# Products without a reader in the opening of a Fourier-mixing and SoLU kernel, with exponents, table zeros and a mean row moved

## The chip, the cores and the metric

The kernel runs on one core of one Trainium2 chip. The metric is the device time of one execution in microseconds (us). A profile is one execution recorded instruction by instruction; its times count from the start of its span. The engines are TensorE (PE, with its weight loads listed apart as PEld), VectorE (DVE), ScalarE (ACT), GpSimd (POOL) and SyncE (SP, whose queue issues most DMAs).

## The reference

For x of shape 8 x 3136 x 256, each batch is Fourier transformed over the sequence and over the features, and the real part is kept. Each of the 25,088 rows then passes a small network:

```
X = fft(fft(x, axis=1), axis=2).real          # rows of 256
h = X @ w_in                                   # 256 x 1024
e = exp(h - max(h));  solu = h * e / sum(e)
ln = (solu - mean) / sqrt(var + 1e-6) * g_ln   # mean and var over the 1024
out = ln @ w_out                               # 1024 x 256
```

w_in, w_out and g_ln are random. Here w_in and w_out arrive as 64-bit floats, and the kernel converts them to 32 bits itself, in the opening.

## The kernel before

**The work.** The batches are taken in four pairs. For each pair the sequence transform of length 3136 = 49 x 64 is split in two: a first transform over 49 (`transform1`), and a second over 64 (`transform2`). The features' transform is folded into the weights: the kernel computes `Wi`, the product of the Fourier table Q and w_in, once, in the opening. After that it works through 100 units of 128 rows (25 per pair). For each unit PE computes the second transform (L245), ACT copies its result to q (L251), PE multiplies q by `Wi` in an even and an odd half (`up`, L281), DVE joins the halves (L294, L302), ACT takes exponents and squares, DVE the products (L317), and the result is turned and multiplied by `Wo`. The even half needs `w_mid`, a further row of weights.

**The opening.** The first pair is loaded in eight pieces (c = 0 to 7). A piece needs a direct load (xa, or `room` for pieces 2 to 5, issued by SP) and an indexed load of its mirror image (xb, issued by POOL). DVE adds the two (`add_mirror`, L145 and L147), folds the features (`fold`, L152, L153, L165) into a buffer y, of which there are two, so that the fold of piece c + 2 waits until PE has read piece c. `transform1` (L217) multiplies y by the table F in two steps of four calls; each call appears in the profile as two records. ACT copies each step's result (L220), SP stores it to a scratch tensor zd, and when all eight pieces are there, `turn` reads it back as g, which `transform2` needs.

**The weights in the opening.** w_in comes in four pieces of 512 columns (raw_in). `exponent_in(i)` takes a piece's exponents on DVE (L586) and confines them in three steps on ACT (L610, L612, L614, in `confine`); `narrow_in(i)` builds the 32-bit numbers on DVE in four instructions (L586, L627, L630, L636), of which L630 needs the confined exponents. `product_in(h)` (L690) makes the two halves of `Wi` and the middle row on PE, in PSUM tiles of tags h0 and h1; `keep_in` copies them out (L694). w_out is converted in the same way (`exponent_out`, `narrow_out`). `mean_out(0)` (L737) multiplies a matrix of ones by the first half of `Wo`, four calls of 256 columns, and `mean_out(1)` adds the second half later; `keep_mean` copies the sum out as the mean row. `T`, the table of the second transform, is zeroed at L820 before its two blocks are loaded (L675).

**What sets the order.** The schedule is manual: each engine takes its instructions in the order in which the program lists them, and semaphores order them between engines. The loop over c in the main body gives, for each piece: conversion of a piece of w_in (c = 0: pieces 0 and 1, c = 1: piece 2), `add_mirror`, in c = 0 and c = 2 the exponents of w_in's pieces 2 and 3, `fold`, in c = 2 the conversion of piece 3, the load of piece c + 6, in c = 3 the issue of w_out's load and of the first table, then `transform1`, and from c = 3 on parts of `product_in`. After the loop come the rest of `product_in`, the last exponents, `mean_out(0)`, and for units 0 and 1 `transform2`, `take2` (L251) and `spread`. `begin(i)` issues for a unit both calls of `up` with `even` (L294) between them, and `second_transform(i + 2)`. The loop over units calls `begin(1)` after the exponentials of unit 0 and before its product.

Of the kernel before, what the change touches and what calls it, by code (L numbers as in the profile page):

```python
# [9 lines left out]
FP32 = mybir.dt.float32  # L10
# [7 lines left out]
P = 128  # L18
# [26 lines left out]
def kernel(  # L45
# [19 lines left out]
    nc = tc.nc  # L65
    B, S, D = x.shape
    FF = moe_w_in.shape[1]
# [16 lines left out]
    ps_h = ctx.enter_context(tc.tile_pool(name="ps_h", bufs=1, space=PSUM))  # L84
# [11 lines left out]
    ident = const.tile([P, P], FP32, name="ident")  # L96
# [21 lines left out]
    def load(pr, c, room=None):  # L118

        r = slice(pr.p * PR, (pr.p + 1) * PR)  # L120
        rows = PR if pr.p else P
        if room is None:
            xa = xpool.tile([P, CH, D], FP32, tag="xa", name="xa")
            xb = xpool.tile([P, CH, D], FP32, tag="xb", name="xb")
        else:
            xa, xb = (t.rearrange("p (l d) -> p l d", d=D) for t in room)
        nc.sync.dma_start(out=xa[0:rows], in_=x_pn[r.start : r.start + rows, c * CH + 1 : (c + 1) * CH + 1, :])
        i = pr.p * NC + c
        nc.gpsimd.indirect_dma_start(
            out=xb[0:rows].rearrange("p l d -> p (l d)"), out_offset=None, in_=x_g,  # L130
            in_offset=bass.IndirectOffsetOnAxis(ap=idx[0:rows, i : i + 1], axis=0))
        xa, xb = xa[0:PR], xb[0:PR]
        x0 = None
        if c == NC - 1:
            x0 = xpool.tile([PR, 1, D], FP32, tag="x0", name="x0", bufs=1)
            nc.sync.dma_start(out=x0, in_=x_pn[r, 0:1, :])
        pr.raw[c] = (xa, xb, x0)

    def add_mirror(pr, c, engine, part=None):

        xa, xb, _ = pr.raw[c]
        rows = (0, CH) if part is None else (part * CH // 2, (part + 1) * CH // 2)
        r = slice(rows[0], min(rows[1], CH - 1 if c == NC - 1 else CH))
        a, rb = xa[:, r, :], xb[:, ::-1, :][:, r, :]
        i = engine.tensor_tensor(out=a[:, :, 1:D], in0=a[:, :, 1:D], in1=rb[:, :, D - 1 : 0 : -1], op=ALU.add)  # L145
        if part is None:
            engine.tensor_tensor(out=a[:, :, 0:1], in0=a[:, :, 0:1], in1=rb[:, :, 0:1], op=ALU.add)  # L147
        return i
# [6 lines left out]
    def fold(pr, c):  # L155

        xa, _, x0 = pr.raw.pop(c)
        pr.y[c] = xpool.tile([PR, CH, D], FP32, tag="y", name="y")
        sides = [(pr.y[c], xa)]
        if c == NC - 1:  # L160
            pr.y0 = xpool.tile([PR, 1, D], FP32, tag="y0", name="y0", bufs=1)
            sides.append((pr.y0, x0))
        for o, i in sides:
            fold_features(o, i)
            nc.vector.tensor_copy(out=o[:, :, 0:129:128], in_=i[:, :, 0:129:128])  # L165
# [406 lines left out]
    NW = 512  # L572
# [25 lines left out]
    def confine(unit, here=False, parts=(0, 1, 2)):  # L598

        if unit is None:  # L600
            return
        if here:
            bits(unit, unit, -896.0, ALU.add, 0.0, ALU.max)
            bits(unit, unit, 255.0, ALU.min, 2.0 ** 23, ALU.mult)
            return

        u = unit.bitcast(FP32)
        for i in parts:
            if i == 0:
                nc.scalar.activation(out=u, in_=unit, func=ACT.Relu, bias=limits[:, 0:1])  # L610
            elif i == 1:
                nc.scalar.activation(out=u, in_=u, func=ACT.Relu, bias=limits[:, 1:2], scale=-1.0)  # L612
            else:
                nc.scalar.activation(out=unit, in_=u, func=ACT.Identity, bias=limits[:, 2:3], scale=-(2.0 ** 23))  # L614
# [24 lines left out]
    class Weights:  # L639
# [43 lines left out]
        def product_in(self, h, parts=range(4), ps=None):  # L683
# [6 lines left out]
                nc.tensor.matmul(ps[:, fs], lhsT, self.w_in[c][:, fs], start=(c == 0), stop=(c == KD - 1))  # L690
            return ps

        def keep_in(self, h, ps):
            nc.scalar.copy(w_mid if h == KD else Wi[:, h, :], ps)  # L694

# [95 lines left out]
    with tc.manual_schedule():  # L791
        pairs = [Pair(p) for p in range(NP)]
        first, weights = pairs[0], Weights()
# [23 lines left out]
        for i, limit in enumerate((-896.0, 255.0, 255.0 * 2.0 ** 23, 1e-12)):  # L817
            nc.vector.memset(limits[:, i : i + 1], limit)
        for t in T:
            nc.vector.memset(t, 0.0)  # L820
        weights.exponent_in(0)
        weights.exponent_in(1)
        for c in range(NC):

            if c == 0:
                weights.narrow_in(0)
                weights.narrow_in(1)
            elif c == 1:
                weights.narrow_in(2)
            add_mirror(first, c, nc.vector)  # L830
            if c in (0, 2):
                weights.exponent_in(2 + c // 2)
            fold(first, c)
            if c == 2:
                weights.narrow_in(3)
            if c == NC - 1:
                for i in range(2):
                    weights.exponent_out(i)
                confine(weights.units[0], True)
                weights.narrow_out(0)  # L840
            if c + 6 < NC:
                load(first, c + 6)
            if c == 3:
                weights.place_out()
                for i in range(2):
                    weights.load_out(i)
                weights.load_table(0)
                weights.scale_out()
            for s in range(CH // 2):
                if c == NC - 1:  # L850
                    confine(weights.units[0], parts=(s,))
                transform1(first, c * CH // 2 + s)
            if c == 3:
                weights.mid()
                weights.keep_in(0, weights.product_in(0))
            elif c == 4:
                odd = weights.product_in(1, (0,))
            elif c == 5:
                weights.product_in(1, (1,), odd)
# [13 lines left out]
        units = [Unit(p, k1) for p in range(NP) for k1 in range(NK)]  # L873
        for i in (1, 2):
            weights.narrow_out(i)
        weights.mean_out(0)
        pairs_q = [(t, transform2(pairs[0], t.k1, t.k1)) for t in units[:2]]
        confine(weights.units[0], parts=(0, 1))
        for (t, ps), part in zip(pairs_q, ((2,), ())):
# [29 lines left out]
        def begin(i):  # L909

            cur = units[i]
            enter(i)
            ps = up(cur, 0)
            if i in (2, 3):
                column(cur)
            even(cur, ps)
            cur.odd = up(cur, 1)
            second_transform(i + 2)

        def other_pairs(i, do, *a):  # L920
            cur = units[i]
            if cur.p + 1 < NP:
                do(pairs[cur.p + 1], i, *a)

        batches = []
        begin(0)
        for i in range(whole + 1):
            cur = units[i]
            prv = units[i - 1] if i else None
            if prv:  # L930
                turn_whole(prv, i == 1)
            if i == 1:
                weights.mean_out(1)
            for s in cur.signs:
                join(cur, s)
            if i == 0:
                weights.narrow_out(3, (2,))
                weights.fold_out()
            if 1 < i < whole:
                for o, ps in prv.wait:  # L940
                    nc.vector.tensor_copy(out=o, in_=ps)
            for s in cur.signs:
                expo(cur, s)
            if i == 1:
                weights.keep_mean()
            if i in (1, whole):
                for o, ps in prv.wait:
                    nc.scalar.copy(o, ps)
            if i == 0:
                begin(1)  # L950
            done = units[0 if i == 2 else i - 1 : i] if i > 1 else []
            for t in done:
                stats(t)
            if i == whole:
                nxt = units[i + 1]
                enter(i + 1)
                even(nxt, up(nxt, 0))
            if i == whole:
                other_pairs(i, ahead, "fold")
            for s in cur.signs:  # L960
                product(cur, s)
                if i < whole and s == 0:
                    square(cur, s)
            if i == 1:
                weights.centre(cur)
            if i == 2:
                weight_sums(cur)
            if i < whole:

                if i:  # L970
                    begin(i + 1)
                if 1 in cur.signs:
                    square(cur, 1)
            else:
                for s in cur.signs:
                    square(cur, s)
                other_pairs(i, ahead, "mirror", cur)
                sums(units[1], None, part=slice(2, 4))
                turn_both(cur)
                stats(cur)  # L980
            for work in ("mirror", "fold", "load") if i < whole else ("load",):
                other_pairs(i, ahead, work, cur)
            if i == whole - 1:
                sums(units[1], None, part=slice(0, 2))
            for t in done:
                power(t)
# [185 lines left out]
```

## Time and profile before

| what | value |
|---|---|
| median of three executions | 1125.55 us (1125.4 to 1126.89) |
| the profiled execution | 1126.52 us |
| its span, first to last instruction | 1124.6 us |
| mean granted clock of TensorE | 0.995 of full |
| PE busy | 1093.9 us (97%) |
| DVE busy | 980.1 us (87%) |
| ACT busy | 798.3 us (71%) |
| POOL busy | 802.6 us (71%) |
| first product on PE | 16.44 us |
| first product of `up` | 57.88 us |

In the order of time, a line gives start and length in us, engine, line of the program, operation, output<-input by the program's names, size and number of records, and in brackets the idle time of the engine before it and what ended it. A line with several records is merged: its length reaches from the start of the first to the end of the last. PE's records overlap, so the distance of two starts says more than a length. In a table of stretches, a line gives the stretch, its length, the busy us (and records) of PE, PEld, DVE, ACT and POOL, the clock that TensorE was granted (1.00 is full), the mean busy share of the DMA engines and what they moved in GB/s.

### The profile page before, as it was taken

What the parts mean: (1) busy time and instruction counts of PE and PEld (TensorE: products, weight loads), DVE (VectorE), ACT (ScalarE), POOL (GpSimd) and SP (SyncE); (2) the same over time, 40 slices, a digit from 0 to 9 for tenths busy, and PEclk for the clock granted to TensorE, in tenths of its full rate; (3) what the DMA queues carried; (4) which work ended last, traced back from release to release, by engine and by line L of the source; (5) the groups of instructions that cost most, each with busy time, mean ns of one, the idle gap of its engine ahead of it and who ended that gap; (6) DMA issues with size and microseconds to landing.
All of it is one profiled execution on the core that took longest, in us unless ns stands there. A gap on an engine that the chain in (4) does not pass through costs nothing. (4 is left out here: it accounts for less than half of the span.)

```text
span 1124.6 us, 22003 instructions
## 1 busy us (share of the span) xinstructions
PE 1093.9 (97%) x7031; PEld 874.4 (78%) x7031; DVE 980.1 (87%) x1440; ACT 798.3 (71%) x1946; POOL 802.6 (71%) x707
## 2 busy tenths in 40 slices
PE   3899999999999999999999999999999999999998
PEld 2556878787787787878877787878877788778888
DVE  7899889889889888898888988898988899888984
ACT  4478777777766777777767777777776777777771
POOL 3058888776777888865877788876776676766665
PEclk9899999999999999999999999999999999999999
DMA  9473798766978889766988797776786785865665
GB/s 350 170 202 85 175 188 199 179 145 151 172 174 164 203 178 190 193 146 141 163 171 178 173 194 186 192 178 143 153 154 145 139 163 124 157 145 112 141 136 125
DMA packets 457929, 187.74 MB, mean 167 GB/s; under 512 B 424646, under 2 KB 439254, under 8 KB 457816
## 3 DMA queue, kind: packets, MB, share of 16 engines
q1 hardware_dynamic: 443800, 146.94, 61.7%
q0 software_dynamic: 14016, 39.40, 13.0%
q8 instruction: 57, 0.93, 0.4%
q14 instruction: 56, 0.46, 0.1%
HBM read 46.75 MB, written 38.80 MB: 76 GB/s over the span
## 5 line engine op out<-in xcount | busy, mean ns | idle before, releaser
L281 PE MATMUL ps_h<-Wi,q 128*128 128x512 f32 x800 | 361.6, 593 | 0.5 <-DVE nmax L302 0.2
L457 POOL TENSOR_TENSOR S<-uT 128x512 f32<-128x512 f32 x186 | 237.6, 1278 | 111.0 <-DVE u L317 30.7
L464 PE MATMUL ps_m<-Ws,S 128*128 128x128 f32 x2304 | 296.1, 275 | 0.0
L464 PEld LDWEIGHTS ps_m<-Ws,S 128*128 128x128 f32 x2304 | 279.5, 192 | 3.4 <-DVE S L457 0.2
L324 ACT ACTIVATE h<-u,usum 128x1024 f32<-128x1024 f32 x196 | 224.9, 1148 | 71.5 <-DVE u L317 71.3
L281 PEld LDWEIGHTS ps_h<-Wi,q 128*128 128x128 f32 x800 | 144.2, 190 | 145.0 <-issue 141.9
L317 DVE SCALAR_TENSOR_TENSOR u<-h,u 128x1024 f32<-128x1024 f32 x196 | 232.9, 1224 | 10.7 <-ACT u L310 10.6
L310 ACT ACTIVATE u<-h,nmax 128x1024 f32<-128x1024 f32 x196 | 223.2, 1141 | 2.3 <-DVE nmax L302 1.1
L388 DVE STREAM_TRANSPOSE v<-u 128x2048 f32<-128x2048 f32 x88 | 203.4, 2311 | 3.0
L464 PE MATMUL ps_m<-Wo,uT 128*128 128x128 f32 x1536 | 203.7, 276 | 0.0
L464 PEld LDWEIGHTS ps_m<-Wo,uT 128*128 128x128 f32 x1536 | 187.9, 192 | 1.0 <-issue 1.0
L302 DVE CUSTOM_DVE_ANT_0 h<-ev,ps_h 128x1024 f32<-128x1024 f32 x100 | 122.1, 1221 | 17.1 <-DVE ev L294 9.3
L302 DVE CUSTOM_DVE_ANT_0 h<-h,ps_h 128x1024 f32<-128x1024 f32 x96 | 117.2, 1221 | 14.6 <-DVE nmax L302 0.5
L551 POOL DMA_INDIRECT out_dram<-ot,idx x96 | 107.5, 1120 | 27.6 <-issue 10.2
L457 POOL TENSOR_TENSOR S<-uT,S 128x512 f32<-128x512 f32 x93 | 118.9, 1279 | 7.2
L457 POOL TENSOR_TENSOR S<-S,uT 128x512 f32<-128x512 f32 x93 | 118.7, 1277 | 7.3
L294 DVE SCALAR_TENSOR_TENSOR ev<-w_mid,r,ps_h 128x1024 f32<-128x1024 f32 x99 | 122.8, 1240 | 0.9 <-PE ps_h L281 0.7
L464 PE MATMUL ps_m<-Ws,uT 128*128 128x128 f32 x768 | 101.8, 276 | 0.0
L464 PE MATMUL ps_m<-Wo,S 128*128 128x128 f32 x768 | 101.4, 275 | 0.0
L245 PEld LDWEIGHTS ps_m<-T,g 128*128 128x128 f32 x400 | 60.1, 191 | 47.3 <-issue 45.9
L217 PE MATMUL ps_m<-y,F 98*100 98x258 f32 (+3 forms) x288 | 71.8, 384 | 24.5 <-DVE y L165 22.8
L499 ACT ACTIVATE ot<-ps_m,rs 128x256 f32<-128x256 f32 x96 | 45.5, 474 | 70.6 <-PE ps_m L464 50.6
(111 smaller groups left out, 1232.9 us busy)
## 6 DMA issues: line engine op xcount, KB each, us to landing
uT<-v SPq DMA_DIRECT2D x752, 128.0 KB
g<-zd POOLq DMA_DIRECT2D x72, 160.0 KB, 5.3
out_dram<-ot SPq DMA_DIRECT2D x176, 64.0 KB
zd<-z SPq DMA_DIRECT2D x24, 400.0 KB
xa<-in_x_dram SPq DMA_DIRECT2D x24, 392.0 KB
raw_in<-in_moe_w_in_dram SPq DMA_DIRECT2D x4, 512.0 KB
xa<-in_x_dram SPq DMA_DIRECT2D x4, 512.0 KB
room<-in_x_dram SPq DMA_DIRECT2D x4, 512.0 KB
```

The source lines that it names most:

```text
L217: nc.tensor.matmul(o[..., cs], F[:, 2 * t + h, :], i[..., cs], start=first, stop=True, skip_group_check=True)
L245: nc.tensor.matmul(o, g[:, k, h * P : (h + 1) * P], table, start=(h == 0), stop=True, skip_group_check=True)
L281: nc.tensor.matmul(ps[:, fs], t.q[:, c * P : (c + 1) * P], Wi[:, c, fs], start=True, stop=not whole_even)
L294: nc.vector.scalar_tensor_tensor(out=t.ev, in0=w_mid, scalar=t.r, in1=ps, op0=ALU.mult, op1=ALU.add)
L302: nc.vector.tensor_tensor_reduce(out=t.h[s], in0=t.h[0] if s else t.ev, in1=t.odd, scale=1.0 if s else -0.5, scalar=3.0e38, op0=ALU.add, o ...
L310: nc.scalar.activation(out=t.u[s], in_=t.h[s], func=ACT.Exp, bias=t.nmax[:, s : s + 1], scale=-1.0, accum_out=t.esum[:, s : s + 1])
L317: t.last = nc.vector.scalar_tensor_tensor(out=t.u[s], in0=t.h[s], scalar=-1.0, in1=t.u[s], op0=ALU.mult, op1=ALU.mult, accum_out=t.usum[:, ...
L324: nc.scalar.activation(out=t.h[s], in_=t.u[s], func=ACT.Square, bias=t.usum[:, s : s + 1], scale=-float(FF), accum_out=t.ssq[:, s : s + 1])
L388: nc.vector.transpose(out=t.batch.v[:, :, t.w], in_=t.both.rearrange("p s (g n) -> p (s g) n", n=32))
L457: i = engine.tensor_tensor(out=S[j], in0=a, in1=b, op=op)
L464: nc.tensor.matmul(o, a[:, c], b[:, c], start=start and c == 0, stop=c == n - 1, skip_group_check=True)
L551: dma = nc.gpsimd.indirect_dma_start(out=out, out_offset=bass.IndirectOffsetOnAxis(ap=idx[:, i : i + 1], axis=0), in_=t.ot[s], in_offset=None)
```

## The change

Four edits, all of them in the opening:

- A new function `busy(n)` multiplies `ident` by the first 512 columns of w_in, n times, into a PSUM tile of tag h0. Nobody reads the result. It is called before `transform1` of pieces 0 to 3, with n = 12, 2, 1 and 4.
- `exponent_in(3)` moves from piece 2, between `add_mirror` and `fold`, to piece 1, after `fold`.
- The two zero fills of T move from DVE to GpSimd, at the same place in the program.
- `mean_out(0)` moves from ahead of the first `transform2` to behind `begin(0)`.

```diff
+        def busy(self, n):
+            ps = ps_h.tile([P, FF], FP32, tag="h0", name="busy")
+            for _ in range(n):
+                nc.tensor.matmul(ps[:, 0:NW], ident, self.w_in[0][:, 0:NW], start=True, stop=True)
+
...
         for t in T:
-            nc.vector.memset(t, 0.0)
+            nc.gpsimd.memset(t, 0.0)
...
             add_mirror(first, c, nc.vector)
-            if c in (0, 2):
-                weights.exponent_in(2 + c // 2)
+            if c == 0:
+                weights.exponent_in(2)
             fold(first, c)
-            if c == 2:
+            if c == 1:
+                weights.exponent_in(3)
+            elif c == 2:
                 weights.narrow_in(3)
...
                 weights.scale_out()
+            if c < 4:
+                weights.busy((12, 2, 1, 4)[c])
             for s in range(CH // 2):
...
         for i in (1, 2):
             weights.narrow_out(i)
-        weights.mean_out(0)
         pairs_q = [(t, transform2(pairs[0], t.k1, t.k1)) for t in units[:2]]
...
         begin(0)
+        weights.mean_out(0)
         for i in range(whole + 1):
```

## Prediction

> **What bounds the kernel now.** I read the busy totals first, then the opening alone.
>
> ```profile
> PE 1093.9 (97%) x7031; PEld 874.4 (78%) x7031; DVE 980.1 (87%) x1440; ACT 798.3 (71%) x1946; POOL 802.6 (71%) x707
> ```
>
> TensorE (PE) is busy 1093.9 of 1124.6 us; 22.8 us of its 30.7 idle us are three waits before 32.24 us (16.44, 1.31 and 5.06). So from the end of the opening on, PE has hardly a gap: what the opening loses or wins should reach the end nearly whole. PE in order of time:
>
> ```profile
> 16.44 3.73 PE L217 MATMUL ps_m<-y,F 98*100 98x258 f32 x8 [16.44 <-DVE y L165]
> 21.49 5.54 PE L217 MATMUL ps_m<-y,F 98*100 98x258 f32 x16 [1.31 <-DVE y L165]
> ...
> 32.24 3.71 PE L217 MATMUL ps_m<-y,F 98*100 98x258 f32 x8 [5.06 <-DVE y L165]
> 35.74 5.17 PE L690 MATMUL wps<-w_in,Q 128*128 128x512 f32 x8
> 40.75 1.89 PE L217 MATMUL ps_m<-y,F 98*100 98x258 f32 x8
> ```
>
> The eight records of one piece (L217) take 3.7 us early and 1.89 at 40.75. The clock explains it; here are the busy times and the granted clock in stretches of 3.41 us:
>
> ```profile
> 25.25:28.66 3.41, 1.93 (x9) 1.18 (x8) 0.65 (x1) 3.33 (x6) 0.00 (x0) 1.00 1.03 397
> 28.66:32.07 3.41, 0.00 (x0) 0.00 (x0) 3.35 (x8) 0.35 (x2) 0.00 (x0) 0.50 0.94 366
> 32.07:35.48 3.41, 3.24 (x8) 2.31 (x9) 3.38 (x7) 0.59 (x1) 0.00 (x0) 0.50 0.61 221
> 35.48:38.90 3.42, 3.42 (x6) 1.52 (x5) 2.97 (x7) 1.18 (x3) 0.00 (x0) 0.50 0.97 352
> 38.90:42.31 3.41, 3.41 (x13) 1.94 (x12) 0.00 (x0) 1.36 (x2) 0.00 (x0) 1.00 0.39 141
> 1117.51:1120.93 3.42, 2.49 (x22) 2.29 (x21) 0.83 (x2) 0.53 (x2) 0.96 (x1) 1.00 0.00 0
> ```
>
> A stretch with PE busy 1.93 of 3.41 us was followed by half clock; one with 3.24 at half clock did not bring it back, one with 3.42 did. Near the end 2.49 busy of 3.42 did not lose it. Before 25.25 the column has no record; the 3.73 us of the first piece say half clock. The 5.06 us gap comes from VectorE:
>
> ```profile
> 28.01 0.75 DVE L630 SCALAR_TENSOR_TENSOR S<-raw_in,top_bit,S 128x512 int32<-128x512 int32 x1 [2.84 <-ACT S L614]
> ...
> 42.68 0.69 DVE L152 TENSOR_TENSOR y<-xa 98x508 f32<-98x508 f32 x1 [4.13 <-PE ps_m L217]
> ```
>
> At 28.01 it had waited 2.84 us for the exponents of w_in's last piece, at 42.68 it waits 4.13 us for a y buffer, that is for PE. From 32.24 to 57.8 PE sets the pace. How that stretch ends (PE, then ACT, then DVE):
>
> ```profile
> 51.55 3.60 PE L690 MATMUL wps<-w_in,w_mid 128*128 128x512 f32 x8
> 54.98 1.89 PE L737 MATMUL ps_m<-Wo,ones 128*128 128x256 f32 x8
> 56.71 1.05 PE L245 MATMUL ps_m<-T,g 128*128 128x128 f32 x8
> 57.88 3.70 PE L281 MATMUL ps_h<-Wi,q 128*128 128x512 f32 x8
> ...
> 61.87 3.60 PE L281 MATMUL ps_h<-Wi,q 128*128 128x512 f32 x8
> ```
>
> ```profile
> 55.19 1.01 ACT L694 COPY w_mid<-wps 128x1024 f32<-128x1024 f32 x1 [0.29 <-PE wps L690]
> 56.09 0.72 ACT L610 ACTIVATE S<-S,limits 128x512 f32<-128x512 int32 x1
> 56.85 0.72 ACT L612 ACTIVATE S<-S,limits 128x512 f32<-128x512 f32 x1
> 57.48 0.35 ACT L251 COPY q<-ps_m 128x256 f32<-128x256 f32 x1
> ```
>
> ```profile
> 63.79 1.28 DVE L294 SCALAR_TENSOR_TENSOR ev<-w_mid,r,ps_h 128x1024 f32<-128x1024 f32 x1
> ```
>
> The mean row (L737) fills PE while ScalarE (ACT), without a break after its wait at 55.19, keeps w_mid, does two steps of exponents and then copies q, which `up` (57.88) needs. Without L737, q would still not come before 57.48.
>
> **The skill.** "TensorE: Matmul & The Clock Gate", Part 1, says that the clock is halved until a busy window of about 3.4 us has passed, and that these windows run free of the kernel's start. The trace agrees (0.215 against 0.43 us a record; changes at 25.25, 28.66 and 38.90). Its summary "Why this matters for your kernels" allows PE gaps of up to about 3 us; here 1.5 us idle within one stretch (27.2 to 28.66) was enough, and the measurement decides. The same page (Part 1, engine queue depths) calls ACT and DVE strictly first in, first out: the q copy, queued behind the exponents, agrees. For the memsets, "GPSIMD Engine Reference", 3.1, gives 1.03 cycles an element for one-input bodies (quoted at 1.2 GHz); only a 128x128 memset, 0.21 us, is in the trace.
>
> **The added products.** One call of 512 columns is two records of 0.43 us (0.857), twice that at half clock. The first needs `ident` (1.3 us) and w_in's first 512 columns, written by the L636 step that ends at 9.32; PE starts at 9.37. The counts 12, 2, 1 and 4 are 10.28, 1.71, 0.86 and 3.43 us at full clock: 16.28. With four pieces of `transform1` (4 x 1.72 = 6.88), the gain transpose (0.15) and `product_in(0)` (3.43), PE has 26.74 us of work ahead of piece 4's transform, plus C/2, where C is the time at half clock: from 3.4 (a window begins at 9.37) to 6.8 us, middle 5.1. So piece 4 starts at 9.37 + 26.74 + C/2 = 36.11 + C/2 = 37.8 to 39.5, middle **38.7**, against 40.75: **a gain of 2.05 us** (2.9 to 1.2). This holds if data never come later than PE. The first y is there at 16.44, but the twelve products end at 19.65 + C/2 = 22.2: PE is late, not DVE. Piece 2's fold waits for piece 0's y buffer (two buffers), to 22.2 + 1.9 = 24.1 instead of 22.75. Piece 3's y is there at about 31.0 (next part); PE reaches it at 33.5. So 2.5 us of the added products are pure delay, and they hide every smaller change on DVE.
>
> **Exponents sooner.** The step is one DVE instruction (0.34 us of its row) and three ACT ones (2.25). They move ahead of piece 1's two copies on ACT: these wait until 26.8, but PE finishes piece 1 only at 27.4, so nobody waits for the DMA behind them either. ACT gets to the exponents after piece 0's copies (24.6), is done at 26.8, and DVE's L630, due at 26.55, starts at 26.9; piece 3's y, 4.08 us later as in the trace, comes at 31.0 instead of 32.1. With this edit alone undone, the exponents would follow piece 1's copies (28.1) to 30.3, y would come at 34.4 and cost 0.9 us; as it is, the edit is worth nothing beyond the sum above. On SP's queue, piece 0's store to zd goes from 20.8 to 24.7, and piece 7's load behind it from 21.46 to 25; it landed at 32.8, so some 36.4, and is used after 41.
>
> **Table zeros.** DVE's two memsets (0.59 + 2.19) were followed by a 0.41 us wait for raw_in: nothing gained. On GpSimd they stand behind the index loads (10.65): 3,200 elements are about 2.7 us by the skill's price (an estimate), 8 by the 128x512 additions' 1278 ns. They end between 13.4 and 18.7, so piece 6's indexed load (14.91) slips by 0 to 3.8 us. It lands at 28, is used at 37: worth 0. I take 2.7.
>
> **The mean row later.** Eight records of 0.215, 1.72 us, leave PE ahead of `transform2`; by the ACT rows above this gains 0, since q waits for ACT. Put after `begin(0)`, they lie between the third `transform2` and `up` of unit 1 (61.87). Its first half ends at 63.7, which is when L294 starts (63.79); DVE was free at 63.65. So L294 waits: behind it on DVE are the product of unit 0 and all that follows, and PE's transposes wait for that product. DVE has hardly a gap up to 98 us to make it good. **Cost 1.66 us** (0 if it is made good later).
>
> **Sum.** 1126.52 (profiled run; span 1124.6 and 1.9 around it) - 2.05 + 1.66 = **1126.1**; with C from 3.4 to 6.8, 1125.3 to 1127.0. The profiled run lies 0.97 above the median 1125.55 of three (1125.4 to 1126.89). It got its clock back 6.7 us after 32.24, near the latest phase, and each us there costs 0.5; at another phase the kernel before is up to 1.6 us shorter. Against the median my sum is 0.5 us slower, under the 0.2% (2.25 us) that a measurement can tell from no change.
>
> **Rivals.** *The clock is lost again* (ends slower). With the mean row gone, PE idles from 55.1 until g lands (about 56.2, by the DMA events), and from the end of the two `transform2` (57.3) to 57.88: some 1.7 us of 2.8, all shifted alike. The clock was lost with 1.48 idle us in a stretch and kept with 0.93. Where a window covers most of the gap, half clock follows for one or two windows: 1.7 to 3.2 us, middle 2.4, on `up`, which is on the path. Time 1128.5. It decides if more than about 1.2 idle us in a window is enough, and then for some phases, perhaps half. *The mean row's cost is made good*: PE has about 1.5 idle us between 60 and 100 (38.49 busy of 40 in stretches of ten); then 1126.1 - 1.66 = 1124.4. Against it: DVE's rows follow each other. *The products start later*, after the second half's conversion (11.8) if the wait covers the whole w_in tile: +2.45, 1128.6. Against it: the mean row at 54.98 read Wo while L636 still wrote other columns of it at 56.4.
>
> **How the numbers follow.** Sum as above 0.56; clock lost 0.25; made good 0.12; later start 0.07. Faster by over 0.2% (below 1123.3) needs the made-good case at its luckiest: 0.03. Slower (above 1127.8): 0.25 and 0.05 of the last. The range, 1124.4 to 1128.9, takes in half of the made-good case and most of the slow ones.
>
> **What would show it.** Right: PE busy without a gap from 9.4 to about 53, full clock from 13 to 16 us on, piece 4's L217 at 37.8 to 39.5, L610 to `up` as now, L737 ahead of unit 1's `up`, and L294 of unit 1 waiting some 1.6 us for PE. Wrong: a wait for y in that stretch, q sooner after w_mid than 2.3 us, or unit 1's L294 not waiting.

## The result, and the profile after

The changed kernel takes 1126.88 us (median of 22 executions, 1126.07 to 1130.56), the kernel before 1125.32 (22 executions, 1123.71 to 1126.89). The ratio is 1.0015, 95% interval 1.0009 to 1.0021: 0.15% slower, or 1.56 us. The forecast was 1126.1 (1124.4 to 1128.9), within 0.2% of before; the measured time is 0.8 us above it. The profiled execution of the changed kernel took 1126.33 us (span 1124.6), 0.55 under its median; that of before had taken 1126.52, 1.2 above its own.

PE of the changed kernel in order of time; these lines answer to the L217, L690, L737 and L281 lines of before (L737 is now L742, L694 is L699, and L696 is `busy`):

```profile
9.55 12.75 PE L696 MATMUL busy<-w_in,ident 128*128 128x512 f32 x24 [9.55 <-DVE w_in L636]
22.14 1.89 PE L217 MATMUL ps_m<-y,F 98*100 98x258 f32 x8
...
33.69 1.89 PE L217 MATMUL ps_m<-y,F 98*100 98x258 f32 x8
35.42 3.60 PE L690 MATMUL wps<-w_in,Q 128*128 128x512 f32 x8
38.85 1.89 PE L217 MATMUL ps_m<-y,F 98*100 98x258 f32 x8
...
49.66 3.60 PE L690 MATMUL wps<-w_in,w_mid 128*128 128x512 f32 x8
54.52 1.13 PE L245 MATMUL ps_m<-T,g 128*128 128x128 f32 x8 [1.27 <-DMA g<-zd]
55.99 3.70 PE L281 MATMUL ps_h<-Wi,q 128*128 128x512 f32 x8 [0.34 <-ACT q L251]
59.53 0.61 PE L245 MATMUL ps_m<-T,g 128*128 128x128 f32 x4
59.98 1.89 PE L742 MATMUL ps_m<-Wo,ones 128*128 128x256 f32 x8
61.70 3.60 PE L281 MATMUL ps_h<-Wi,q 128*128 128x512 f32 x8
```

No idle time is listed between 9.55 and the end of L690: PE works without a gap, and every piece takes 1.89 us, the length at full clock. Piece 4 (third L217 line) starts at 38.85 instead of 40.75, and `up` of unit 0 at 55.99 instead of 57.88: 1.9 us sooner. But `up` of unit 1, behind L742, starts at 61.70 instead of 61.87. DVE shows the two ends of this, a wait for a y buffer early and for unit 1's `up` late, with the exponents between them:

```profile
24.07 0.69 DVE L152 TENSOR_TENSOR y<-room 98x508 f32<-98x508 f32 x1 [2.11 <-PE ps_m L217]
...
26.82 0.75 DVE L630 SCALAR_TENSOR_TENSOR S<-raw_in,top_bit,S 128x512 int32<-128x512 int32 x1 [0.33 <-ACT S L614]
```

```profile
60.88 0.88 DVE L636 SCALAR_TENSOR_TENSOR Wo<-raw_out,g_ln,S 128x256 f32<-128x256 f32 x2
63.62 1.28 DVE L294 SCALAR_TENSOR_TENSOR ev<-w_mid,r,ps_h 128x1024 f32<-128x1024 f32 x1 [1.87 <-PE ps_h L281]
```

The 2.84 us wait for the exponents has shrunk to 0.33, yet 2.11 us of waiting for PE stand ahead of it: VectorE did not get ahead; it now waits for TensorE instead of ScalarE. And where L294 of unit 1 followed L636 at once, it now waits 1.87 us. ACT between w_mid and q is as before, only 1.9 us sooner:

```profile
53.29 1.01 ACT L699 COPY w_mid<-wps 128x1024 f32<-128x1024 f32 x1 [0.29 <-PE wps L690]
54.20 0.72 ACT L610 ACTIVATE S<-S,limits 128x512 f32<-128x512 int32 x1
54.96 0.72 ACT L612 ACTIVATE S<-S,limits 128x512 f32<-128x512 f32 x1
55.59 0.35 ACT L251 COPY q<-ps_m 128x256 f32<-128x256 f32 x1
```

From w_mid to q it is 2.30 us, against 2.29 before. Taking the mean row away from PE there has moved nothing.

How much of a shift in the opening reaches the end? For each record of `up` (800 in either kernel) I subtracted its start before from its start in the profile named; the last column is the difference of the two profiled executions' times:

```
us against before   record 1   record 9   record 401   record 800   whole time
changed kernel        -1.89      -0.16       -0.13        -0.13        -0.19
e1, row back          -0.73      -0.73       -0.72        -0.72        -0.77
e2, row late alone    -2.13      +1.30       +1.32        +1.32        +1.25
e3, exponents alone   -3.44      -3.44       -3.42        -3.43        -3.41
e7, fewer, row late   -5.71      -3.99       -3.99        -3.99        -3.46
e9, seven             -6.18      -6.18       -6.17        -6.10        -5.15
```

Record 9 is the first of unit 1. From there on a shift stays to within 0.1 us over a thousand us in these six; only behind the last `up` do two of them give back 0.5 and 1.0. In the profiles of e4 and e6 it moved by 0.1 on the way, in that of e10 by 0.35. So the start of unit 1's `up` tells what a profiled execution is worth, to about 1 us.

### The profile page after: what moved, and what is told of

The parts are those of the page before. It is cut to its first block, busy times and chain, and to the rows that moved or that the text cites. A ratio compares the mean times of both kernels' runs of the same rounds, so it can differ in the third digit from the quotient of the medians.

```text
span 1124.6 us, 22083 instructions
## 1 busy us (share of the span) xinstructions
PE 1105.5 (98%) x7069; PEld 878.8 (78%) x7069; DVE 977.8 (87%) x1438; ACT 798.4 (71%) x1946; POOL 809.2 (72%) x709
## 5 line engine op out<-in xcount | busy, mean ns | idle before, releaser
L281 PE MATMUL ps_h<-Wi,q 128*128 128x512 f32 x800 | 361.6, 593 | 0.7 <-ACT q L251 0.3
L281 PEld LDWEIGHTS ps_h<-Wi,q 128*128 128x128 f32 x800 | 144.3, 190 | 145.3 <-issue 142.2
L294 DVE SCALAR_TENSOR_TENSOR ev<-w_mid,r,ps_h 128x1024 f32<-128x1024 f32 x99 | 122.9, 1241 | 2.7 <-PE ps_h L281 2.6
L464 PEld LDWEIGHTS ps_m<-Ws,uT 128*128 128x128 f32 x768 | 93.8, 192 | 0.0
```

Of the source, the lines that this page charges most:

```text
L281: nc.tensor.matmul(ps[:, fs], t.q[:, c * P : (c + 1) * P], Wi[:, c, fs], start=True, stop=not whole_even)
L294: nc.vector.scalar_tensor_tensor(out=t.ev, in0=w_mid, scalar=t.r, in1=ps, op0=ALU.mult, op1=ALU.add)
L464: nc.tensor.matmul(o, a[:, c], b[:, c], start=start and c == 0, stop=c == n - 1, skip_group_check=True)
```

## The experiments

All ratios are to executions of the kernel before run beside them. The theory is the prediction's sum; the rivals are named in each expectation. e1 to e4, e5 to e8 and e9 to e11 ran on three chips, where the kernel before took 1125.12, 1125.37 and 1125.43 us, so a difference across these groups is rougher than one within.

**e1: the changed kernel with the mean row back in its old place.**

```diff
+        weights.mean_out(0)
         pairs_q = [(t, transform2(pairs[0], t.k1, t.k1)) for t in units[:2]]
...
         begin(0)
-        weights.mean_out(0)
```

> The changed kernel with the mean row back ahead of the first second transform. Theory of the sum (the row was free in the gap that PE has there while ACT copies q, and costs 1.7 us where it stands now, because unit 1's even half on DVE waits for it): 1.75 us less than the changed kernel, about 1125.1, within 0.3 us of the kernel before; up of unit 1 starts 1.7 us sooner after up of unit 0 than in the changed kernel. Rival (the row's cost is made good later; the loss comes from the added products): the time of the changed kernel, about 1126.9.

Measured: 1125.23 us, ratio 0.9999 (0.9990 to 1.0007). It is 1.65 us under the changed kernel's 1126.88 (1.8 by the ratios), and the rest of the change, together, is worth nothing that can be measured. In its profile `up` of unit 1 follows that of unit 0 after 3.98 us (57.16 and 61.14), against 5.71 in the changed kernel. So the sum holds for the row, and the rival, that its cost is made good later, falls.

**e2: the mean row moved, nothing else.**

```diff
-        weights.mean_out(0)
         pairs_q = [(t, transform2(pairs[0], t.k1, t.k1)) for t in units[:2]]
...
         begin(0)
+        weights.mean_out(0)
```

> The kernel before with only the mean row moved behind begin(0). Theory of the sum: 1.7 us slower than before, about 1127.0, with DVE's even half of unit 1 waiting 1.7 to 1.9 us for PE. Rival (made good later): as before, 1125.3. Rival (the clock is lost in the gap before up): 1128 to 1130, with half clock in the records after 57 us.

Measured: 1127.32 us, ratio 1.0023 (1.0016 to 1.0029), 2.2 us above before (1125.12). The move alone costs what was expected and somewhat more. Its profile shows where more can come from; here are PE's last lines of the opening, and three stretches of it (columns as before, the granted clock third from the end):

```profile
49.42 3.60 PE L690 MATMUL wps<-w_in,w_mid 128*128 128x512 f32 x8
54.02 1.13 PE L245 MATMUL ps_m<-T,g 128*128 128x128 f32 x8 [1.00 <-DMA g<-zd]
55.76 5.40 PE L281 MATMUL ps_h<-Wi,q 128*128 128x512 f32 x8 [0.61 <-ACT q L251]
```

```profile
52.77:56.19 3.42, 1.81 (x10) 1.26 (x10) 3.32 (x7) 3.10 (x5) 0.71 (x2) 1.00 0.39 125
56.19:59.60 3.41, 3.41 (x5) 1.35 (x4) 1.18 (x3) 0.40 (x2) 0.00 (x0) 0.50 0.32 60
59.60:63.01 3.41, 3.41 (x16) 2.41 (x15) 2.69 (x5) 0.93 (x2) 0.00 (x0) 1.00 0.64 127
```

A stretch with 1.61 idle us is followed by one at half clock, and `up` of unit 0 takes 5.40 instead of 3.70 us. The prediction's rival of a lost clock is real in this kernel, in this execution. The mean granted clock was recorded for every execution; a stretch of 3.41 us at half clock lowers it by 0.0015 (half of 3.41 in 1125). Nine of the 21 executions have 0.997 and a median of 1126.83, 1.7 us above before; the other twelve have 0.995 or 0.996 and 1127.85. That fits the lost clock, but the gap before piece 3 costs the clock in this kernel too (before itself has 0.995 to 0.997), so the figures don't separate the two losses.

**e3: the exponents of w_in's last piece moved, nothing else.**

```diff
-            if c in (0, 2):
-                weights.exponent_in(2 + c // 2)
+            if c == 0:
+                weights.exponent_in(2)
             fold(first, c)
-            if c == 2:
+            if c == 1:
+                weights.exponent_in(3)
+            elif c == 2:
                 weights.narrow_in(3)
```

> The kernel before with only the exponents of w_in's last piece moved. Theory of the sum (without the added products VectorE sets the pace until piece 3, so the 2.84 us wait at L630 is on the path): the wait is gone, piece 3 reaches PE near 29.3 instead of 32.2, and the time falls by 2.5 to 3.3 us, to about 1122.5. Rival (PE or the loads take the place of that wait, as they do in the changed kernel): within 0.5 us of before.

Measured: 1122.61 us, ratio 0.9977 (0.9969 to 0.9984): 2.5 us faster. The edit that was forecast at nothing beyond the sum in the company of the others is the best of them alone. PE and one line of DVE of its profile:

```profile
28.85 3.71 PE L217 MATMUL ps_m<-y,F 98*100 98x258 f32 x8 [2.23 <-DVE y L165]
32.35 5.12 PE L690 MATMUL wps<-w_in,Q 128*128 128x512 f32 x8
37.30 1.89 PE L217 MATMUL ps_m<-y,F 98*100 98x258 f32 x8
```

```profile
24.63 0.75 DVE L630 SCALAR_TENSOR_TENSOR S<-raw_in,top_bit,S 128x512 int32<-128x512 int32 x1
```

L630 no longer waits. Piece 3 comes 3.4 us sooner than before (28.85 against 32.24), still at half clock (3.71), and that is the shift that stays to the end. Not all of it is due to the exponents: piece 0 came 1.1 us sooner in this execution (15.35 against 16.44), as it did in e2 (15.37), which lacks this edit and reaches piece 3 at 31.16. The 2.3 us between 31.16 and 28.85 agree with the 2.5 of the medians.

**e4: the added products, nothing else.**

```diff
+            if c < 4:
+                weights.busy((12, 2, 1, 4)[c])
             for s in range(CH // 2):
```

> The kernel before with only the added products (12, 2, 1, 4). Theory of the sum: full clock from 13 to 16 us on, but piece 0 reaches PE only at about 22, and the exponents of the last piece come behind piece 1's copies, at 30.3, so that PE waits about 0.9 us for piece 3; the clock won and the time spent nearly cancel: 0.5 us slower than the median of before, about 1125.8 (1125.0 to 1126.5). Rival (the clock alone is worth 1.5 to 2 us of the opening): about 1123.5.

Measured: 1126.56 us, ratio 1.0011 (1.0004 to 1.0018), 1.4 us above before (1125.12) where 0.5 was expected (1125.0 to 1126.5 us). The rival (the clock alone gains) falls. PE and DVE of the profile, whose execution took 1127.52, 1.0 above the median:

```profile
10.93 13.39 PE L696 MATMUL busy<-w_in,ident 128*128 128x512 f32 x24 [10.93 <-DVE w_in L636]
24.16 1.89 PE L217 MATMUL ps_m<-y,F 98*100 98x258 f32 x8
...
36.51 1.94 PE L217 MATMUL ps_m<-y,F 98*100 98x258 f32 x8 [0.64 <-DVE y L165]
38.29 3.60 PE L690 MATMUL wps<-w_in,Q 128*128 128x512 f32 x8
41.73 1.89 PE L217 MATMUL ps_m<-y,F 98*100 98x258 f32 x8
```

```profile
32.28 0.75 DVE L630 SCALAR_TENSOR_TENSOR S<-raw_in,top_bit,S 128x512 int32<-128x512 int32 x1 [3.77 <-ACT S L614]
```

With late exponents L630 waits 3.77 us and PE 0.64 for piece 3, much as worked out (0.9). The surprise is the first line: the products started at 10.93, not 9.37, as VectorE had the first piece of w_in at 6.38 instead of 4.98 (its first L586 on raw_in).

**e5: the zero fills on GpSimd, nothing else.**

```diff
         for t in T:
-            nc.vector.memset(t, 0.0)
+            nc.gpsimd.memset(t, 0.0)
```

> The kernel before with only the two zero fills on GpSimd. Theory of the sum (VectorE waits for the first piece of w_in after its fills anyway, and GpSimd is free when it takes them): no change, 1125.1 within 0.4 us; VectorE's wait for raw_in grows to about 4 us and its first exponents start when they did. Rival (the fills hold up GpSimd's index loads or the loads of the first piece): a difference of 0.5 us or more either way, with piece 0's mirror at another time than 12.3 to 13.3 us.

Measured: 1125.72 us, ratio 1.0004 (0.9996 to 1.0013): no change, as expected. In its profile VectorE waits 4.14 us for raw_in and starts its exponents at 5.37.

**e6 and e7: fewer first products, with the mean row back (e6) and late (e7).** Both are the changed kernel with this edit, and e6 has that of e1 as well:

```diff
-                weights.busy((12, 2, 1, 4)[c])
+                weights.busy((4, 2, 1, 4)[c])
```

> The changed kernel with the mean row back and counts 4, 2, 1 and 4 instead of 12, 2, 1 and 4. Theory of the sum (eight of the first twelve products were pure delay of PE, 8 x 0.857 us, and VectorE sets the pace again until piece 3): PE takes piece 3 as soon as VectorE has it, at 28.5 to 29.5, already at full clock, and piece 4 at 33.7 to 34.7; about 3 us under the kernel with the exponents alone (1122.6), 1119.5 (1118.8 to 1120.5). Rival (the added products bring nothing once the exponents are early; DVE or the loads bind later): 1122 to 1123. Rival (with four products the clock is lost in the gaps between pieces): half clock in the records between 20 and 35, 1121 to 1123.

> The changed kernel with only the counts changed, 4, 2, 1 and 4. Theory of the sum (edits add up): the mean row's 1.7 to 2.2 us above the kernel of the same call that has the row back, about 1121.4 (1120.8 to 1122.2). Rival (the row's place matters only where PE sets the pace from 9 us on): no difference between the two.

Measured: e6 1121.78 us, ratio 0.9970 (0.9960 to 0.9979); e7 1123.98, ratio 0.9991 (0.9983 to 0.9999). By medians, and by the lowest executions (1120.09 and 1122.27), the row's place costs 2.2 us here too, so the rival named for e7, no difference, falls. But both missed their expected times, e6 1119.5 by 2.3 us and e7 1121.4 by 2.6. The twelve executions of e6 fall into two groups, seven from 1120.1 to 1122.2 and five from 1123.4 to 1124.6; those of e7 reach from 1122.3 to 1125.6, with one at 1128.25. The profile of e6, 1124.56 us, is from its upper group:

```profile
10.40 6.03 PE L696 MATMUL busy<-w_in,ident 128*128 128x512 f32 x8 [10.40 <-DVE w_in L636]
18.57 3.73 PE L217 MATMUL ps_m<-y,F 98*100 98x258 f32 x8 [2.15 <-DVE y L165]
```

```profile
15.14:18.56 3.42, 1.28 (x3) 0.19 (x1) 3.42 (x8) 1.40 (x2) 1.48 (x1) 1.00 1.03 417
18.56:21.97 3.41, 3.40 (x8) 2.45 (x9) 3.34 (x6) 1.36 (x3) 0.00 (x0) 0.50 1.02 407
21.97:25.38 3.41, 3.41 (x5) 1.34 (x5) 3.38 (x9) 2.05 (x4) 1.20 (x1) 0.50 1.03 412
```

Four products were over 2.15 us before piece 0's y came; the clock was lost at 18.56 for two stretches, and the next products ran at half clock and held PE back. The rival with the clock is what happened in this execution. It does not explain the whole upper group: the profiled execution has a mean granted clock of 0.996, but three of the other four have 0.999, as the lower group has. These cannot have lost the clock once they had it. The mean does not count half clock before the first grant (the changed kernel ran at half clock up to 14.00 and has 0.999), so they may have been granted full clock later; no trace shows it, and their cause is open.

**e8: the mean row late, two products without a reader in its old place.** The kernel before with the move of e2, `busy` with its tile under tag h1, and:

```diff
+        weights.busy(2)
         pairs_q = [(t, transform2(pairs[0], t.k1, t.k1)) for t in units[:2]]
```

> The kernel before with the mean row moved behind begin(0), and two products without a reader (1.71 us, PSUM tag h1) in the row's old place. Theory that the row costs 1.73 us of the path and a further 0.4 to 0.5 us by executions in which the idle gap costs the clock: the gap is gone, so 1126.85, and no execution above some 1128.6. Rival (the clock in the gap does not matter; the move alone costs 2.2 us): 1127.3, as with the row moved alone.

Measured: 1126.86 us, ratio 1.0013 (1.0007 to 1.0020), no execution above 1128.31, where the highest of e2 was 1129.60. The intervals of e2 and e8 overlap, so this points to the lost clock as the rest of e2's 2.2 us without settling it. Its profile keeps full clock there, and `up` of unit 0 takes 3.70 us.

**e9: seven first products, row back.** The changed kernel with e1's edit and:

```diff
-                weights.busy((12, 2, 1, 4)[c])
+                weights.busy((7, 2, 1, 4)[c])
```

> The changed kernel with the mean row back and counts 7, 2, 1 and 4. With four first products the profile lost the clock in the 2.15 us gap before piece 0 and its executions fell into two groups, 1120.1 to 1122.2 and 1123.4 to 1124.6. Theory (seven products end at 15.5 to 18, when piece 0's y comes, so the gap and with it the upper group go, and PE still reaches piece 3 no later than VectorE's y, near 29): 1120.5 (1119.8 to 1121.3), no group above 1123. Rival (the upper group comes from late loads, not from the clock): 1121.8 and two groups as with four.

Measured: 1121.37 us, ratio 0.9962 (0.9949 to 0.9976), five executions from 1120.53 to 1122.05, all at a mean granted clock of 0.999 or 1.000, and none in an upper group. Five are few: with e6's share of seven in twelve, all five would fall into the lower group about one time in fifteen (an estimate), and their median lies in e6's lower group. It has the lowest median of all, 4.1 us under before and 5.6 under the changed kernel run beside it, though 0.9 above the expected value. Its interval overlaps that of e3, so how much the products add to the early exponents is not settled. PE of its profile:

```profile
9.50 7.72 PE L696 MATMUL busy<-w_in,ident 128*128 128x512 f32 x14 [9.50 <-DVE w_in L636]
17.06 1.89 PE L217 MATMUL ps_m<-y,F 98*100 98x258 f32 x8
18.79 1.88 PE L696 MATMUL busy<-w_in,ident 128*128 128x512 f32 x4
20.88 1.97 PE L217 MATMUL ps_m<-y,F 98*100 98x258 f32 x8 [0.21 <-DVE y L165]
...
34.56 1.89 PE L217 MATMUL ps_m<-y,F 98*100 98x258 f32 x8
```

The first products end at 17, as y comes, and PE waits 0.21 us for piece 1 instead of making it wait. Piece 4 starts at 34.56, 4.3 us before the changed kernel's.

**e10 and e11: the changed kernel with the gap filled, and the changed kernel again.** e10 adds, with the tile's tag as a parameter of `busy`:

```diff
+        weights.busy(2, "h1")
         pairs_q = [(t, transform2(pairs[0], t.k1, t.k1)) for t in units[:2]]
```

> The changed kernel with two more products without a reader (PSUM tag h1) in the mean row's old place. Theory (the changed kernel does not lose its clock in the gap ahead of up: 21 of its 22 executions lie within 1.8 us, about what the phase of the clock's windows makes, and its profile kept full clock with 1.27 idle us in one stretch): the time of the changed kernel run beside it, within 0.3 us. Rival (executions that lose the clock there make part of the loss): 0.4 us or more under it.

> The changed kernel itself, beside the two others. 1126.9; 6.4 us above the kernel with seven products and the row back if the theory of the sum holds: 1.7 for the row and 4.7 for PE's delay by the first five superfluous products (4.3) and by the clock.

Measured: e10 1126.81 us, ratio 1.0012 (1.0006 to 1.0019); e11 1126.99, ratio 1.0014 (1.0007 to 1.0020). Filling the gap changes nothing that can be measured in the changed kernel. The granted clock says the same: all 42 executions of the changed kernel (22 and e11's 20) have a mean of 0.999 or 1.000, where one more stretch at half clock would leave at most 0.998. So the clock is not what it lost. e11 lies 5.6 us above e9, where 6.4 was expected.

## Why the prediction was right, and which term was off

**The path was right.** "Piece 4 starts at 36.11 + C/2": the profile has C = 14.00 - 9.55 = 4.45, which gives 38.3, and 38.5 with its own start at 9.55; measured 38.85. The profiled execution came within 0.2 us of the forecast partly because small misses cancel: it starts 0.2 later, C is 0.65 shorter than the 5.1 of the middle (worth 0.3), and piece 4 comes 0.3 later than the formula gives. The range of C was too narrow at its lower end: it was 2.98 in e9, not at least 3.4. The other steps came out close:

| step | forecast | profile |
|---|---|---|
| piece 2's fold waits until | 24.1 | 24.07 |
| L630 starts (waits) | 26.9 (0.35) | 26.82 (0.33) |
| PE reaches piece 3 | 33.5 | 33.69 |
| piece 7's load on SP | 25 | 25.08 |
| two zero fills on GpSimd | 2.7 us | 2.82 us |
| w_mid to q on ACT | 2.3 us | 2.30 us |
| unit 1's L294 waits | 1.6 us | 1.87 us |

**The mean row** was forecast to gain 0 where it left and to cost 1.66 where it went. In the changed kernel it costs 1.73 by the trace (from 1.89 to 0.16 us of lead) and 1.65 by medians (e1). By itself it costs 2.2 (e2), and 1.5 with its gap filled (e8).

**The exponents** were forecast at nothing in this company, at 0.9 if left undone: the two kernels that differ by the exponents and the neutral zero fills, e4 and e1, are 1.3 us apart. Alone they gain 2.5 (e3): the added products had hidden about half of that.

**The term that was mis-sized** is "a gain of 2.05 us" for the added products with full clock. Against the profile of before it measured 1.90. Against the median it is about nothing: e1, which has the other three edits without the row's move, is at 0.9999. Two things lie behind this. First, the profiled execution of before lay 1.2 us above its median. The prediction saw that it was slow and put this down to the phase of the clock, yet took the gain against it. The phase is one part: from piece 3 to piece 4, where it counts, before took 8.51 us and e2, e3, e5 and e8 7.46 to 8.50. Another part was overlooked: piece 0 came to PE at 16.44 in that execution, and at 15.27 to 15.81 in those four, which begin with piece 0 as before does. A slow base makes the gain look large; it does not shift the forecast time, because what follows piece 4 takes as long whenever it starts.

Second, 9.37 for the first product was a single execution's value, and this does shift the time. The eight profiles with added products ahead of piece 0 start at 9.46 to 10.93, 9.9 in the mean: 0.5 us more, and since PE of the changed kernel then has no gap until 53 us, it reaches the end. Its own profile, with a start at 9.55, lies 0.55 under its median. In sum: 1.90, less 1.2 and 0.55 for where the two profiles lie in their executions, leaves 0.15 of the gain; the row takes 1.7; 1.55 us slower, where the medians say 1.56. That the phase and the late piece 0 make up the 1.2, and the start the 0.55, is inferred from the profiles, as the other executions have no trace.

**The lost clock**, at 0.25, did not occur in the changed kernel's profile (1.27 idle us from 51.55 to 54.96, clock kept), and neither e10 against e11 nor the granted clock of its 42 executions shows it. It did occur in e2. The one execution of 1130.56 us has a mean granted clock of 1.000, so a clock lost again is not what made it long; what did is not known. The later start behind the whole tile did not occur: PE began 0.15 us after L636's first part. That part of the added products was pure delay is shown by e9, but the 2.5 us of the prediction are too few: with five fewer, piece 4 starts 4.3 us sooner, all of their 5 x 0.857 us. The prediction set PE against a y of piece 3 at 31.0, and that y had itself waited for PE (the 2.11 us at L152); in e9 piece 3 starts at 29.40.

**What stays open** is why e9 missed its expectation by 0.9 us. Its profile kept its 6.1 us of lead up to the last `up` and lost 1.0 behind it; PE there waited 1.0 us for a transfer of turned blocks (uT). Whether that wait comes from the shift or by chance was not tried. Open too is what made three of e6's slow executions slow at a full mean clock.

## What to carry to other kernels

Work that keeps TensorE's clock up is paid in TensorE's own time: count it in the same sum as the wait that it fills, and end it where the first real operand arrives; seven first products against twelve were worth 3.9 us by medians (e9 against e1, on two chips). An edit's worth depends on which engine sets the pace beside it, so undo and try the parts one at a time: here one part of four was a gain of 2.5 us under the loss of two others. And before moving work out of a stretch, ask who would use the time; the row lay in a gap that ScalarE made, and went to a place where VectorE waits for every product.

## What the runs showed of the hardware that was not expected

- TensorE lost its clock after stretches of 3.41 us with far less than a whole idle one: 2.13 idle us (e6, in a single gap of 2.15), 1.61 (e2), 1.48 (before). It kept it with 1.27 (changed kernel) and, near its end, with 1.49 (e4, 1119.19 to 1122.60). The busy share alone does not decide: full clock came back after a stretch that was 0.87 busy with 128-row products (e9, 9.06 to 12.48), but not after ones 0.95 and 0.996 busy with 98-row products (before, 32.07 to 35.48; e6, 18.56 to 21.97). It did come after one wholly busy with 98-row products (before, 21.83 to 25.25). Whether the rows used or something else makes the difference was not tried.
- The same first 512 KB load (w_in's first piece) was there for VectorE at 4.82 to 6.38 us in the profiles (e11 and e4), with no load ahead of it that differed between the kernels.
- Executions of one kernel spread over nearly 4 us (before: 1123.4 to 1127.2 in 170 executions), and a kernel whose TensorE never idles in the opening over less (the changed one 1126.0 to 1128.1, but for one at 1130.6). A single profile is a poor base for a forecast of one us.
